# Token rows turned by VectorE in 32x32 squares, stored and gathered as four pieces a token

## The chip, the cores and the metric

The kernel runs on one core of a Trainium2 chip. The metric is the device time of one execution in microseconds; three runs of the kernel before gave 716.85, 718.15 and 718.57 us, so its median is 718.15 us. All data is float32.

## What is computed

Sliding-window attention with ALiBi biases, and behind it a mixture of experts that sends each token to one expert. Cut to what matters:

```python
# attention: 8 batches, 8 heads, 576 positions, 64 per head
mask = (rel >= 0) & (rel < 128)                    # rel = query position - key position
attn = softmax(where(mask, q @ k.T / 8 - slope[h] * |rel|, -1e9))
x = (attn @ v) as rows of (batch, position)        # 4608 tokens x 512
# experts: 8, each 512 -> 1024 -> 512
logits = x @ w_gate                                # 4608 x 8
e = argmax(logits, 1);  g = softmax(logits)[e]
y[t] = g[t] * (relu(x[t] @ w1[e]) @ w2[e])
```

## The kernel before, in words

**Order.** One instruction stream for each engine, in an order that is written out by hand (`manual_schedule`). What the program issues first for an engine runs first on it, so an instruction that waits holds up all that stands behind it on its engine. Two lists of small functions, `tasks` and `fill`, are dealt out between the large steps: `some()` and `step()` each take one entry (itself a list of functions) from the front.

**Attention** (lines 1192 to 1228). 4 pairs of batches (`bp`) x 4 pairs of heads (`hp`) make 16 units of 4 steps, so 64 steps `i`. In a step, TensorE computes the scores of step i+2 (L749), ScalarE takes their exponential (L755), VectorE multiplies by the bias factors (L758, L763), and TensorE multiplies the probabilities of this step with the values (L784). Twice a unit `finish` copies the result into `xT[bp]` (ScalarE, L801 and L803; features on partitions, 1152 tokens in columns) and sums the probabilities (TensorE L816 into a bank of the two-bank pool `ps_m`, VectorE L827 into `sumT`). One pool of two PSUM banks, `ps_m`, serves all the small products.

**Routing of a pair of batches** is dealt out over the 16 steps of the next pair, by `behind(bp)`: `gate` (L836, L841) and `turn` (L860) give gate logits with tokens on partitions; `scale_a`, `scale_b`, `scale_c` (VectorE, L869 to L923) give the softmax sums, the chosen expert and for each token and head one scale, into `K["ext"]`; `count`, `place` (L930, L939), `ones_at` (L968 to L977) and `enlist` (L987, L994) put the token's number into its expert's list. 9 tiles of 128 tokens (`TPB`) are made into rows meanwhile.

**Rows.** `row_turned` turns a tile of 128 tokens with four TensorE transposes (L1001) into a bank of `ps_m`, and ScalarE copies it into `xs` (L1003; pool `rows`, three buffers). `row_out` adds the 16 columns of scales on GpSimd (L1007) and stores rows of 528 numbers from SP's queue (L1009) to `x_rows` in device memory. 36 tiles in all.

**Gathering.** `index` turns lists of token numbers into `g_idx` (rows to read) and `s_idx` (rows to write). `gather` (L1107) issues one indirect DMA on GpSimd for each tile of 128 listed tokens; 39 in all: 4 for each of the 8 experts' fixed groups and 7 for single-tile further groups. `to_scale` (VectorE, L501) multiplies by the scales into `xn`, `to_columns` turns the tile with four TensorE transposes (L1124) into `ps_m`, and ScalarE copies it to `xgT` (L1125). `x_sums` (L537 to L540) and `w1_sums` (L529 to L532) make the sums that Strassen's scheme needs. For expert 0 only the tokens of the first three pairs of batches are taken in the fixed group (`gather(fixed[0], ...)`, the last entry of `behind(2)`), so that its products can begin while the last pair is being routed; its `w1_sums` run in units 10 and 11.

**Experts.** A fixed group of 512 tokens is multiplied by w1 in `strassen1` (seven products m, each in two halves c; 14 steps, L1295) and by w2 in `strassen2` (14 steps, L1352); after each step one `fill` entry is issued. A further group of 128 tokens is done plainly (L1391, L1407). Groups alternate: one fixed, one further. The scaled results are scattered by indirect DMAs (L1375). `with_tail` deals out the routing of the last pair of batches in `strassen1` of the first group, and the gather and preparation of the second group in its `strassen2`; later groups are gathered ahead of `strassen1` and prepared during `strassen2` of the group before.

Of the kernel before, what the change touches and what calls it, by code (L numbers as in the profile page):

```python
# [8 lines left out]
F32 = mybir.dt.float32  # L9
# [6 lines left out]
P = 128  # L16
# [441 lines left out]
def kernel(  # L458
# [36 lines left out]
    RW = Dm + 16  # L495

    x_d = nc.dram_tensor("x_rows", (N, RW), F32, kind="Internal").ap()

    def token_scales(to, rows):

        nc.vector.tensor_tensor(  # L501
            to.rearrange("p (h d) -> p h d", h=H), rows[:, :Dm].rearrange("p (h d) -> p h d", h=H),
            rows[:, Dm : Dm + H].unsqueeze(2).to_broadcast([P, H, D]), op=ALU.mult,
        )

    with ExitStack() as fast:
# [12 lines left out]
        rows = pool(tail, "rows", 3, side="right")  # L519
# [131 lines left out]
        far = ac.tile([P, 2, GC], F32, name="far")  # L651
# [50 lines left out]
        def route_consts():  # L702
# [12 lines left out]
            K["first_w"] = iota("first_w", [P, E], [[-1, E]], E, 0)  # L715
            K["off"] = iota("off", [P, E], [[NS * P, E]], -1, 0)

        def token_numbers():
# [3 lines left out]
            K["ext"] = rte.tile([P, NT, 16], F32, name="ext")  # L722
            nc.gpsimd.memset(K["ext"][:], 0.0)
# [125 lines left out]
        gsr, r_of, pr_of, ex_of, sel_of, pre_of, slot_of = {}, {}, {}, {}, {}, {}, {}  # L849
# [65 lines left out]
        def scale_c(bp):  # L915
            ts = slice(bp * TPB, (bp + 1) * TPB)
# [5 lines left out]
            nc.vector.reciprocal(gw[:], gw[:])  # L922
            nc.vector.tensor_tensor(  # L923
                K["ext"][:, ts, :H].rearrange("p t (h a) -> p t a h", a=2), r[:],
                gw[:].unsqueeze(2).unsqueeze(3).to_broadcast([P, TPB, 2, HP]), op=ALU.mult,
            )

# [36 lines left out]
        def ones_at(bp):  # L964
# [11 lines left out]
            orow = small.tile([P, TPB, P], F32, name="orow")  # L976
# [21 lines left out]
        def row_turned(bp, t):  # L998
            ps = ps_m.tile([P, 512], F32, name="m")
            for hp in range(HP):  # L1000
                nc.tensor.transpose(ps[:, hp * P : (hp + 1) * P], xT[bp][:, hp, t * P : (t + 1) * P], ident[:])  # L1001
            xs = xs_of[bp, t] = rows.tile([P, RW], F32, name="xs")
            nc.scalar.copy(xs[:, :Dm], ps[:])  # L1003

        def row_out(bp, t):
            xs = xs_of.pop((bp, t))
            nc.gpsimd.tensor_copy(xs[:, Dm:], K["ext"][:, bp * TPB + t, :])  # L1007
            for p0, n, r0 in placed(bp, t):
                nc.sync.dma_start(x_d[r0 : r0 + n, :], xs[p0 : p0 + n, :])  # L1009
# [526 lines left out]
```

## Time and profile before

| what | value |
|---|---|
| median of three runs | 718.15 us (716.85 to 718.57) |
| the profiled execution | 721.43 us |
| its span in the trace | 719.7 us |
| TensorE busy | 681.8 us, 6204 matmuls |
| VectorE busy | 343.9 us, 659 instructions |
| ScalarE busy | 225.8 us, 410 instructions |
| GpSimd busy | 112.4 us, 199 instructions |
| DMA | 122.01 MB in 59710 packets, 170 GB/s on average |

The span is what the trace shows from the first instruction to the last; the profiled execution's own time is 1.7 us longer. A line of a group gives the engine, the operation, what is written and read, the count, then the engine's busy time in that group and the mean duration of one, and the idle time just before these instructions with what ended it. Consecutive instructions of an engine overlap a little, so the distance from one to the next can be smaller than a duration. The first fixed group's first product begins at 191.99 us; from 255.3 us on a fixed and a further group together take 64.7 us, seven times over.

### The profile page before, as it was taken

The numbers are of one execution on the slowest core, as the hardware profiler recorded it, in microseconds if no ns is written. First come the engines' busy times: TensorE is split into PE (matmuls) and PEld (weight loads), VectorE is DVE, ScalarE is ACT, GpSimd is POOL, SyncE is SP. The second block draws the span as 40 slices with busy tenths as digits, with TensorE's granted clock in tenths as the row PEclk, the third lists the DMA queues.
The fourth block names the chain that finished last, engine by engine and source line by source line (L and its number), as shares of the span: only waits on it lengthen the run. The fifth ranks groups of instructions, "written<-read, shape, count | busy, mean of one in ns | idle before, by whom it ended". The sixth has DMA issues, their size and how long they took to land.

```text
span 719.7 us, 14743 instructions
## 1 busy us (share of the span) xinstructions
PE 681.8 (95%) x6204; PEld 569.5 (79%) x6204; DVE 343.9 (48%) x659; ACT 225.8 (31%) x410; POOL 112.4 (16%) x199
## 2 busy tenths in 40 slices
PE   6999799979899999999999999999999999999992
PEld 5878678767588888878897887889788888878881
DVE  4558449665558665524553443364254425514310
ACT  5655455444343223213302320331132023213110
POOL 7000101002001140122023002302200230210020
PEclk9999899989999999999999999999999999999997
DMA  8777877764415763184358218533823673182010
GB/s 241 209 215 237 260 225 206 229 175 143 164 75 193 279 242 117 31 296 172 117 169 312 79 55 291 201 117 97 309 93 116 211 278 117 36 297 108 1 61 6
DMA packets 59710, 122.01 MB, mean 170 GB/s; under 512 B 3857, under 2 KB 23345, under 8 KB 59634
## 3 DMA queue, kind: packets, MB, share of 16 engines
q1 hardware_dynamic: 52178, 100.08, 42.7%
q0 software_dynamic: 6304, 20.00, 7.5%
q8 instruction: 51, 0.84, 0.5%
q10 hardware_dynamic: 1152, 0.88, 0.4%
q14 instruction: 25, 0.20, 0.1%
HBM read 101.79 MB, written 19.96 MB: 169 GB/s over the span
## 4 chain that ended last, share of the span: by engine, by line
issue 57%; PE 19%; POOL 10%; DVE 6%; DMA 4%; ACT 2%; POOLq 0%; SPq 0%; DVEq 0%; ACTq 0%
POOL out_dram L1375 5%; PE sp L749 5%; POOL xg L1107 5%; PE at L784 4%; PE m L816 3%; PE m L1001 2%; DVE pe L758 2%; DMA q_sb<-in_qT_dram 2%; PE m L987 1%; PE m L836 1%; ACT pe L755 1%; DMA x_rows<-xs 1%; DMA out_dram<-zo,s_idx 1%; PE pair0b L1295 1%; PE pair0a L1295 1%
## 5 line engine op out<-in xcount | busy, mean ns | idle before, releaser
L1375 POOL DMA_INDIRECT out_dram<-zo,s_idx x39 | 43.9, 1126 | 383.6 <-DVE zo L1366 283.4
L758 DVE TENSOR_TENSOR pe<-pe,fac 128x768 f32<-128x768 f32 x48 | 45.9, 956 | 54.8 <-ACT pe L755 54.8
L749 PE MATMUL sp<-q_sb,k_sb 64*64 64x192 f32 (+2 forms) x1152 | 60.8, 328 | 6.2 <-DMA q_sb<-in_qT_dram 5.4
L755 ACT ACTIVATE pe<-sp 128x768 f32<-128x768 f32 x64 | 51.9, 811 | 45.9 <-PE sp L749 37.6
L784 PE MATMUL at<-pe,v_sb 64*64 64x192 f32 (+2 forms) x1408 | 61.2, 288 | 2.4 <-issue 1.6
L749 PEld LDWEIGHTS sp<-q_sb,k_sb 64*64 64x64 f32 x1152 | 42.7, 141 | 16.0 <-issue 5.1
L784 PEld LDWEIGHTS at<-pe,v_sb 64*64 64x64 f32 x1408 | 46.4, 136 | 11.3 <-issue 6.1
L1107 POOL DMA_INDIRECT xg<-x_rows,g_idx x39 | 42.7, 1095 | 29.8 <-DVE tb L1030 12.6
L1007 POOL COPY xs<-ext 128x16 f32<-128x16 f32 x36 | 12.4, 356 | 180.0 <-DVE ext L923 79.4
L816 PE MATMUL m<-pe,ind 128*32 128x192 f32 (+2 forms) x704 | 30.8, 295 | 6.0 <-ACT xs L1003 4.3
L1125 ACT COPY xgT<-m 128x512 f32<-128x512 f32 x39 | 22.9, 586 | 37.3 <-PE m L1124 36.4
L1306 ACT ACTIVATE h<-h 128x512 f32<-128x512 f32 x32 | 20.2, 631 | 39.5 <-DVE h L1305 32.1
L1003 ACT COPY xs<-m 128x512 f32<-128x512 f32 x36 | 20.6, 584 | 34.4 <-PE m L1001 16.1
L816 PEld LDWEIGHTS m<-pe,ind 128*32 128x32 f32 x704 | 24.2, 113 | 8.4 <-ACT xs L1003 4.4
L501 DVE TENSOR_TENSOR xn<-xg 128x512 f32<-128x512 f32 x39 | 26.2, 686 | 7.0 <-PE m L1124 6.0
L1124 PE MATMUL m<-ident,xn 128*128 128x128 f32 x156 | 23.6, 274 | 2.1 <-DVE xn L501 2.1
L1124 PEld LDWEIGHTS m<-ident,xn 128*128 128x128 f32 x156 | 19.1, 141 | 6.6 <-DVE xn L501 1.4
L1001 PE MATMUL m<-ident,xT 128*128 128x128 f32 x144 | 22.9, 294 | 1.4 <-DVE sumT L827 0.8
L1001 PEld LDWEIGHTS m<-ident,xT 128*128 128x128 f32 x144 | 17.1, 150 | 5.1 <-issue 2.2
L1407 PE MATMUL pair2a<-w,h 128*128 128x512 f32 x48 | 21.1, 592 | 0.0
L801 ACT COPY xT<-at 128x640 f32<-128x640 f32 (+1 forms) x32 | 18.7, 585 | 4.2 <-PE at L784 3.3
L537 DVE TENSOR_TENSOR xs<-xgT 128x512 f32<-128x512 f32 x8 | 5.5, 693 | 27.1 <-ACT xgT L1125 27.1
(355 smaller groups left out, 1371.5 us busy)
## 6 DMA issues: line engine op xcount, KB each, us to landing
w<-in_moe_w_dram SPq DMA_DIRECT2D x29, 2048.0 KB
k_sb<-in_kT_dram SPq DMA_DIRECT2D x15, 576.0 KB
q_sb<-in_qT_dram SPq DMA_DIRECT2D x15, 576.0 KB
v_sb<-in_v_dram SPq DMA_DIRECT2D x30, 288.0 KB
x_rows<-xs SPq DMA_DIRECT2D x32, 264.0 KB
w<-in_moe_w_dram SPq DMA_DIRECT2D x4, 512.0 KB
x_rows<-xs SPq DMA_DIRECT2D x8, 132.0 KB
pace<-pe SPq DMA_DIRECT2D x65, 0.0 KB
```

Source lines behind the costliest of these rows:

```text
L501: nc.vector.tensor_tensor(to.rearrange("p (h d) -> p h d", h=H), rows[:, :Dm].rearrange("p (h d) -> p h d", h=H), rows[:, Dm : Dm + H].uns ...
L749: nc.tensor.matmul(sp[c * KB : (c + 1) * KB, r, c0 : c0 + n], lhsT=k_sb[u][hs, c, kb * KB : (kb + 1) * KB], rhs=q_sb[u][hs, c, kb * KB : k ...
L755: nc.scalar.activation(pe[:], sp[:, :, :GC], AF.Exp, scale=SCALE)
L758: nc.vector.tensor_tensor(pe.rearrange("p r (k c) -> p r k c", k=2), pe.rearrange("p r (k c) -> p r k c", k=2), fac[:, h0 : h0 + 2, None, ...
L784: nc.tensor.matmul(acc[r * D : (r + 1) * D, c, lo - q0 : hi - q0], lhsT=v_sb[u][c * KB : (c + 1) * KB, kb, r * D : (r + 1) * D], rhs=pe[c ...
L816: nc.tensor.matmul(sm[32 * j : 32 * j + 32, lo - q0 : hi - q0], lhsT=none[:] if pe is None else ind[:, hp, :], rhs=fac[:, 0, :KB] if pe is ...
L1001: nc.tensor.transpose(ps[:, hp * P : (hp + 1) * P], xT[bp][:, hp, t * P : (t + 1) * P], ident[:])
L1107: nc.gpsimd.indirect_dma_start(out=g["xg"][:, j, :], out_offset=None, in_=src, in_offset=bass.IndirectOffsetOnAxis(ap=g_idx[:, g["c0"] + j ...
L1124: nc.tensor.transpose(tp[:, db * P : (db + 1) * P], xn[:, db * P : (db + 1) * P], ident[:])
L1125: nc.scalar.copy(g["xT"][:, :, j * P : (j + 1) * P], tp.rearrange("p (d q) -> p d q", d=DB))
L1375: ins = nc.gpsimd.indirect_dma_start(out=out[:, :], out_offset=bass.IndirectOffsetOnAxis(ap=s_idx[:, g["c0"] + j : g["c0"] + j + 1], axis= ...
L1407: nc.tensor.matmul(ps[:], lhsT=g["h"][:, fb, :], rhs=g["w2"][:, fb, :], start=(fb == 0), stop=(fb == FB - 1),)
```

## The change

The transposes leave TensorE. VectorE's own transpose turns squares of 32x32 where they stand, so a tile of 128 tokens x 512 features becomes four squares in each quarter of the partitions: partition 32a+j of `xs[:, k]` holds token 32k+j, and of it the features whose number within 128 lies in quarter a. So a token is stored as four **pieces** of 128 features and 4 scales (132 numbers, 528 bytes) that lie 64 rows apart in `x_pieces`. The gather fetches for each tile four times 128 pieces (`g_idx` gets four columns a tile, by a small product with the constant `to_squares` and six VectorE operations in `pieces`), so that each 32x32 square can be turned back by VectorE straight into `xgT`. The scales are brought onto the right partitions by `spread` (four small products and two ScalarE copies a pair of batches). Rows are stored by GpSimd's queue, one DMA a tile; `rows` has four buffers. The order of the entries changes in `behind`, `with_tail` and the fill of the first `strassen2`; `count_all` is split (`check_all` gets its last part, unchanged); and `prepare(fixed[0])` is issued as a whole at step 61, instead of entry by entry from step 61 on.

```diff
-        rows = pool(tail, "rows", 3, side="right")
+        rows = pool(tail, "rows", 4, side="right")
...
+            sq = K["to_squares"] = rte.tile([P, NA, P], F32, name="to_squares")
...
-                K["ext"][:, ts, :H].rearrange("p t (h a) -> p t a h", a=2), r[:],
-                gw[:].unsqueeze(2).unsqueeze(3).to_broadcast([P, TPB, 2, HP]), op=ALU.mult,
-            )
+                es[:], r[:], gw[:].unsqueeze(2).unsqueeze(3).to_broadcast([P, TPB, 2, HP]), op=ALU.mult,
+            )
+
+        def spread(bp):
+
+            n = TPB * H
+            ps = ps_m.tile([P, 512], F32, name="m")
+            for k in range(NA):
+                nc.tensor.matmul(
+                    ps[:, k * n : (k + 1) * n], lhsT=K["to_squares"][:, k, :],
+                    rhs=es_of[bp].rearrange("p t a h -> p (t a h)"), start=(k == 0), stop=True, skip_group_check=True,
+                )
+            ext = ext_of[bp] = small.tile([P, TPB, NA, HP], F32, name="ext")
+            v = ps[:, : NA * n].rearrange("p (k t a h) -> p a t k h", k=NA, t=TPB, a=2)
+            for a in range(2):
+                nc.scalar.copy(ext[a * KB : (a + 1) * KB], v[a * KB : (a + 1) * KB, a])
...
         def row_turned(bp, t):
-            ps = ps_m.tile([P, 512], F32, name="m")
-            for hp in range(HP):
-                nc.tensor.transpose(ps[:, hp * P : (hp + 1) * P], xT[bp][:, hp, t * P : (t + 1) * P], ident[:])
-            xs = xs_of[bp, t] = rows.tile([P, RW], F32, name="xs")
-            nc.scalar.copy(xs[:, :Dm], ps[:])
+            xs = xs_of[bp, t] = rows.tile([P, NA, PW], F32, name="xs")
+            nc.vector.transpose(
+                xs[:, :, :PD].rearrange("p k (h f) -> p k h f", h=HP),
+                xT[bp][:, :, t * P : (t + 1) * P].rearrange("p h (k j) -> p k h j", j=TQ),
+            )
 
         def row_out(bp, t):
             xs = xs_of.pop((bp, t))
-            nc.gpsimd.tensor_copy(xs[:, Dm:], K["ext"][:, bp * TPB + t, :])
-            for p0, n, r0 in placed(bp, t):
-                nc.sync.dma_start(x_d[r0 : r0 + n, :], xs[p0 : p0 + n, :])
+            nc.gpsimd.tensor_copy(xs[:, :, PD:], ext_of[bp][:, t])
...
+            nc.gpsimd.dma_start(
+                x_blocks[:, b0 : b0 + db + 1 : db, :], xs.rearrange("p (b k) w -> p b (k w)", b=2),
+            )
...
+        def pieces(cols, nm):
+
+            n = cols.stop - cols.start
+            ps = ps_m.tile([P, 512], F32, name="m")
+            for k in range(NA):
+                nc.tensor.matmul(
+                    ps[:, k * n : (k + 1) * n], lhsT=K["to_squares"][:, k, :], rhs=at_of[nm][:],
+                    start=(k == 0), stop=True, skip_group_check=True,
+                )
...
         def gather(g, src):
             nm = "" if g["n"] == NJ else "1"
-            g["xg"] = g["pool"].tile([P, g["n"], RW], F32, name="xg" + nm)
+            g["xg"] = g["pool"].tile([P, g["n"], NA, PW], F32, name="xg" + nm)
             for j in range(g["n"]):
-                nc.gpsimd.indirect_dma_start(
-                    out=g["xg"][:, j, :], out_offset=None, in_=src,
-                    in_offset=bass.IndirectOffsetOnAxis(ap=g_idx[:, g["c0"] + j : g["c0"] + j + 1], axis=0),
-                )
+                for k in range(NA):
+                    nc.gpsimd.indirect_dma_start(
+                        out=g["xg"][:, j, k, :], out_offset=None, in_=src,
+                        in_offset=bass.IndirectOffsetOnAxis(ap=g_idx[:, g["c0"] + j, k : k + 1], axis=0),
+                    )
...
         def to_columns(g, j):
...
-            tp = ps_m.tile([P, 512], F32, name="m")
-            for db in range(DB):
-                nc.tensor.transpose(tp[:, db * P : (db + 1) * P], xn[:, db * P : (db + 1) * P], ident[:])
-            nc.scalar.copy(g["xT"][:, :, j * P : (j + 1) * P], tp.rearrange("p (d q) -> p d q", d=DB))
+            nc.vector.transpose(
+                g["xT"][:, :, j * P : (j + 1) * P].rearrange("p h (k j) -> p k h j", j=TQ), g["xn", j][:],
+            )
...
             if bp == 2:
-                return [g3, t3, a, b + [lambda: row_turned(bp, 0)], c + n + [lambda: row_out(bp, 0)], p + rs[1:3], o + rs[3:5], e + rs[5:7], [early_table] + rs[7:9],
-                        [lambda: gather(fixed[0], x_d[: 3 * 2 * S, :])]]
...
+                return [g3, t3, a, b, c + n + turned[0:1], p + d + outs[0:1] + rs[1:2], o + rs[2:4],
+                        e + [lambda: index(first, listed[:, 0, :NJ], "0")] + rs[4:6],
+                        [early_table, lambda: pieces(first, "0")] + rs[6:9],
+                        [lambda: gather(fixed[0], x_d[: 3 * 2 * S * NA, :])]]
+            return [g3[0:1], g3[1:2], g3[2:] + t3[0:1], t3[1:], a, turned[0:1], b, turned[1:2], c + n,
+                    d + outs, p, rs[2:4], o, rs[4:6], e + rs[6:7], rs[7:9]]
...
-            if u == len(units) - 1 and g == 1:
-                tasks.extend(t for _, t in prepare(fixed[0]))
             if g != 2:
                 some()
+            if i + AHEAD == NG - 1:
+                while tasks:
+                    some()
+                tasks.extend(t for _, t in prepare(fixed[0]))
+                while tasks:
+                    some()
...
+                a, b, c + n, early[0:2], early[2:3] + w[0], p + d + [lambda t=t: row_out(bp, t) for t in range(3)],
+                w[1] + rs[3:4], o, rs[4:6], e + rs[6:8], [table_fixed] + rs[8:9], [lambda: pieces(rest, "1")] + w[2],
             ]
-            self_late.extend(w[6] + w[7])
+            self_late.extend(w2s[3:8])
...
+                for todo in (
+                    [lambda: gather(f1, x_d[:, :]), self_late[0], self_late[1]], [self_late[2], count_all],
+                    [self_late[3], check_all], [self_late[4], table_further], [next_groups],
+                    w1s[0:2], [lambda: pieces(slice(E * NJ, NC), "2")] + w1s[2:4], tokens[0], w1s[4:6], tokens[1], w1s[6:8], tokens[2], [], tokens[3],
+                    later(lambda: x_sums(f1), 4),
+                ):
+                    fill.append((f1, todo))
```

In `to_scale` the product keeps its size (128x512) and its new layout is that of the pieces. `tokens[j]` is `to_scale` and `to_columns` of tile j.

## The prediction, as it was put on record

> **What bounds the kernel now.** I read the page first, then the busy times by stretch, then single stretches in order of time.
>
> ```profile
> span 719.7 us, 14743 instructions
> ...
> PE 681.8 (95%) x6204; PEld 569.5 (79%) x6204; DVE 343.9 (48%) x659; ACT 225.8 (31%) x410; POOL 112.4 (16%) x199
> ...
> L1107 POOL DMA_INDIRECT xg<-x_rows,g_idx x39 | 42.7, 1095 | 29.8 <-DVE tb L1030 12.6
> ...
> L501 DVE TENSOR_TENSOR xn<-xg 128x512 f32<-128x512 f32 x39 | 26.2, 686 | 7.0 <-PE m L1124 6.0
> L1124 PE MATMUL m<-ident,xn 128*128 128x128 f32 x156 | 23.6, 274 | 2.1 <-DVE xn L501 2.1
> ...
> L1001 PE MATMUL m<-ident,xT 128*128 128x128 f32 x144 | 22.9, 294 | 1.4 <-DVE sumT L827 0.8
> ```
>
> TensorE is busy 95% of the span, and the transposes that go are 46.5 us of that. But 48% for VectorE is an average over unlike stages. The busy times by stretch (bounds, length, then PE, PEld, DVE, ACT, POOL, granted clock, DMA) show it:
>
> ```profile
> 56.70:93.40 36.70, 32.29 (x648) 26.76 (x648) 22.04 (x55) 17.67 (x31) 3.24 (x9) 0.91 0.84 255
> ...
> 105.10:136.50 31.40, 30.44 (x679) 25.68 (x671) 27.39 (x63) 17.25 (x31) 3.66 (x9) 1.00 0.75 216
> ...
> 196.40:255.30 58.90, 57.02 (x309) 50.03 (x305) 39.70 (x112) 18.49 (x37) 9.79 (x16) 1.00 0.50 177
> ...
> 320.00:384.70 64.70, 64.70 (x326) 54.55 (x325) 28.03 (x46) 15.47 (x29) 11.42 (x10) 1.00 0.50 172
> ```
>
> In the expert stage (last line) TensorE is never idle and VectorE has half its time free. While the second pair of batches is routed (second line) VectorE works 27.39 of 31.4 us. In the first line TensorE stands 4.26 us (at 71.4, for a ScalarE row copy that waits for the store of `xs`) and then runs at a lower clock:
>
> ```profile
> 75.60:79.00 3.40, 3.35 (x40) 2.59 (x44) 1.31 (x2) 1.84 (x5) 0.20 (x1) 0.50 0.97 313
> ...
> 154.50:158.00 3.50, 3.50 (x30) 3.05 (x34) 2.29 (x10) 1.21 (x3) 1.03 (x3) 0.50 0.33 92
> ```
>
> The clock is 0.50 after that wait and after a 3.7 us wait at 150.8, for some 6.8 us each time: a wait of that length costs 3.4 us more.
>
> **The sizes.** A square transpose on VectorE is not in the trace. Its nearest row is L501, the same 128x512 numbers, at 0.69 us, and 0.60 from start to start in a row of them. Below lies 0.47 (a one-input operation of 128x384 took 355 ns, scaled by 512/384), above 1.35, the longest row of VectorE (L977). I take 0.60 in a chain, the row of the same size. The Trainium skill, "VectorE: DVE Perf Modes", "The three transpose paths", gives 311 ns for 128x128 in bf16 and only squares of 32; four of these would make 1.24 us, an estimate from that page alone, no run here shows it, and it speaks against this change: by it my sum below would end some 17 us above the kernel before.
>
> Four TensorE transposes hold the queue for 0.435 us between other products (241.88 to 242.32 us), and about 0.62 us in the attention (0.66 at 62.06). A small product with `to_squares` is like L987 (18 in 2.18 us): 0.12 us; 16 in `spread` and 12 in `pieces` add 3.4 us. An indirect DMA has a pitch on GpSimd of 1.27 us:
>
> ```profile
> 177.01 1.09 POOL L1107 DMA_INDIRECT xg<-x_rows,g_idx  x1 [5.91 <-DVE pe L758]
> 178.40 0.98 POOL L1107 DMA_INDIRECT xg<-x_rows,g_idx  x1 [0.30 <-issue]
> 179.68 0.95 POOL L1107 DMA_INDIRECT xg<-x_rows,g_idx  x1 [0.30 <-issue]
> 180.94 0.95 POOL L1107 DMA_INDIRECT xg<-x_rows,g_idx  x1 [0.30 <-issue]
> ```
>
> With 2112 and with 2048 bytes a row it is the same (1095 and 1126 ns), so I take it to go with the 128 rows and keep 1.27 for 528 bytes; ends: 0.5 (if a part goes with bytes) and 1.7 (the longest pitch, beside VectorE's work). So a 512-token gather takes 16 x 1.27 = 20.3 us instead of 5.1.
>
> A plain DMA from GpSimd took 0.72 to 0.84 us (gate weights), at most an indirect one's 1.47. With the 0.36 us scale copy, 36 stores are some 42 us on an engine that is idle there; SP's queue loses 40 stores, behind which its paced loads stood. The Trainium skill, "DMA: Bandwidth & Descriptors", "Issuing engine by pattern", calls the SP and ACT queues generally faster, which speaks against this move; with its first-byte figures (about 1 against 0.6 us) a store would land 0.4 us later, 0.4 us once in the sum (the last store before the gather). The trace shows SP's stores held long: a row copy waited 5.8 us for one.
>
> The 75 ScalarE copies (L1003, L1125: 43.5 us) go, off the path, and 8 small ones (like L803, 0.28) come. The constants add four GpSimd selections of at most 0.97 us in the first 20 us, needed after 60 us: nothing. `check_all` only moves.
>
> **Sum, by stage, against the profiled execution (721.43 us).**
>
> *First routed pair (to 93.4).* From 56.7 TensorE needs 32.29 - 3.4 (clock) - 9 x 0.62 + 0.5 = 23.8 us; VectorE 22.04 + 9 x 0.60 = 27.4, with some 2 us of gaps 29.5. VectorE sets the pace; 36.7 become 29.5: **-7.2**, mostly the wait and the slow clock. With four buffers and stores off SP's queue a store has three to four steps (7 to 10 us) to land, against 5.5 us for a DMA under load (the gather issued until 234.5 landed at 239.95).
>
> *Second pair (105.1 to 136.5).* VectorE 27.39 + 5.4 = 32.8 exceeds the 31.4 there are, since the weight sums of expert 0 fall here too: **+1.5**. TensorE's 5.1 us are not earned.
>
> *Third pair, up to the first expert group: the doubtful part.* Now `place` waits for VectorE at 154.5, and the first gather starts at 177.0. After the scan (154.35) VectorE has, up to the last row: nine turned rows 5.4, four probability products 3.5, two sums 0.8, `place` 1.8, `ones_at` 2.5, the list 0.2, `index` and `pieces` 2.2, `early_table` 0.5, together 17 us, and about 2 of waiting while TensorE is at half clock: 174. Copy, issue and landing add 3, so the gather starts at **177, as now** (174 to 180). TensorE's 5 us without rows are again not earned: `enlist` and `pieces` wait for VectorE.
>
> Then 16 DMAs: the 16th is issued by 177 + 20.3 = 197.3 and landed 2.3 us later (now: issued by 181.9, DMA quiet after 184), 199.6. `prepare(fixed[0])` is issued whole at step 61, ahead of the `sumT` additions of steps 62 and 63. So on VectorE they stand behind the last tile: scale and turn 1.25, four sums 2.4, `sumT` 0.9 make 204.2. TensorE's attention work ends by about 187; it does m=1's first half and then stands in `gate`, whose PSUM bank the `sumT` addition has to free.
>
> ```profile
> 191.99 1.89 PE L1295 MATMUL pair0a<-xgT,w 128*128 128x256 f32 x8
> 193.81 1.92 PE L836 MATMUL m<-xT,wgd 128*32 128x512 f32 x16
> ...
> 196.44 1.99 PE L1295 MATMUL pair0b<-xgT,w 128*128 128x256 f32 x8
> ```
>
> The gates take 2.6 us here, so the second half starts at 206.8 instead of 196.44: +10.4, and after such a wait half clock, +3.4: **+13.8**.
>
> *First group's rest.* 9 rows and 4 tiles leave TensorE: 13 x 0.435 = -5.7; 12 small products +1.4; VectorE's added 9 x 0.60 and six list operations, in a chain of adds and routing, +2 (0 to 6). The second gather, 20.3 us of a 24.2 us `strassen2`, lands some 30 us after its start, and the sums are needed at 24.2 + 4 x 1.73 = 31: just hidden. **-2.3**.
>
> *Later groups.* 24 fixed and 7 further tiles, 31 x 0.435: **-13.5**. Cover: 20 gathers are 25.4 us from the start of `strassen1` (24.2 us), and the tiles are turned in the second to fifth step of `strassen2`; VectorE rises from 28.0 to 31 of 62.5 us. If that cover went, VectorE would wait some 5 us a group, without TensorE, which needs its additions only late in `strassen2`.
>
> Sum: -7.2 + 1.5 + 13.8 - 2.3 - 13.5 = -7.7. The profiled execution would take 713.7; since it was 3.3 us above the median of the runs, I put the same difference on the median: 718.15 - 7.7 = **710.4 us**.
>
> **Rivals.**
> *The join is hidden:* pitch under 0.8 us, or gather begun 10 us earlier. Then +13.8 becomes about 0 to 2: 697. For it: ScalarE's copies are gone from the chain; against it: the equal prices of both kinds of indirect DMA.
> *TensorE bounds everywhere:* 36 x 0.62 + 39 x 0.435 - 3.4 = 35.9 us and the waits of 7.7: 675. Against it: the 27.39 of 31.4.
> *Slower: VectorE's transpose is dear.* Each 0.1 us more costs 27 x 0.1 in the attention, where VectorE sets the pace, and some 1.2 in the first group, 3.9 in all. From 0.80 us in a chain the gain is gone; at 1.0 the sum is +7.9 : 726; at 1.35 about 740. For it: no row shows this operation.
> *It does little:* the gathers under weight loads come late in each group too: 31 tiles' gain lost, 718 to 723.
>
> **Numbers.** Forecast 0.42 (703 to 717), hidden join 0.27 (692 to 702), everywhere 0.06, slower 0.20, little 0.05. The range 692 to 728 leaves out the 675 case and the dear end of the slower one. 0.3% is 2.2 us, about what a measurement can tell: faster 0.71, same 0.07, slower 0.22.
>
> **What would show it.** VectorE's transposes at 0.6 to 0.7 us; no half clock near 75; VectorE full from 105 to 136; TensorE idle some 10 us in `gate` before the second half of m=1, with GpSimd's 16 DMAs before it; 62.5 us for each later pair of groups. A gather pitch far from 1.27, or `sumT` ahead of the tiles, would prove me wrong.

## The result: 0.7% slower, and the profile after

The changed kernel takes 722.20 us (median of seven runs, 721.68 to 725.28) beside 718.15 us for the kernel before on the same chip: a ratio of 1.0073, 95% interval 1.0053 to 1.0092. The prediction was 710.4 us and faster. On two other chips the changed kernel took 769 and 770 us, 6.5 to 6.7% more than the kernel before; that is a second matter, and the last group of experiments is about it. Each ratio is taken on one chip.

The page of the changed kernel: the span and the engines' busy times.

```profile
span 721.9 us, 14376 instructions
...
PE 661.7 (92%) x5960; PEld 552.2 (76%) x5960; DVE 394.7 (55%) x749; ACT 186.2 (26%) x343; POOL 256.0 (35%) x360
```

TensorE lost 20 us of work, but the span did not get shorter: it is idle or at half clock for longer. The groups of the new instructions (count, then busy us and mean ns of one, then idle time ahead of them) show that their sizes were as assumed:

```profile
L1165 POOL DMA_INDIRECT xg<-x_pieces,g_idx x156 | 157.7, 1011 | 57.0 <-issue 46.3 <-DVE pick L1118 7.3 <-DMA x_pieces<-xs 2.7
L1184 DVE STREAM_TRANSPOSE xgT<-xn 128x512 f32<-128x512 f32 x39 | 27.7, 711 | 1.3
L1034 POOL DMA_DIRECT2D x_pieces<-xs x36 | 26.3, 730 | 43.0 <-DVE xs L1022 31.6 <-POOL xs L1029 7.2 <-issue 4.2
L1022 DVE STREAM_TRANSPOSE xs<-xT 128x512 f32<-128x512 f32 x36 | 23.8, 689 | 0.4 <-DMA x_pieces<-xs 0.4
```

A transpose on VectorE takes 0.69 to 0.71 us, an indirect DMA 1.0 us with 0.3 us behind it (a pitch of 1.25 us, whether a row has 2112 or 528 bytes), a store from GpSimd 0.73 us. The estimate of 1.24 us from the Trainium skill's page "VectorE: DVE Perf Modes", "The three transpose paths", is not what this kernel shows.

Where the time went, stage by stage (the times are those of the first gates, of the second half of m=1, of the second group's m=1, of the first and last further tile and of the last scatter in the two traces):

| stage | before | after | difference | predicted |
|---|---|---|---|---|
| start to the first pair's gates | 44.03 | 43.38 | -0.7 | 0 |
| first pair routed | 49.29 | 44.70 | -4.6 | -7.2 |
| second pair routed | 43.18 | 48.56 | +5.4 | +1.5 |
| third pair, to the second half of m=1 | 59.94 | 74.66 | +14.7 | +13.8 |
| first group's rest | 58.85 | 56.14 | -2.7 | -2.3 |
| second group, to its further tile | 50.67 | 54.67 | +4.0 | -2.2 (5 tiles x 0.435) |
| the rest, to the last scatter | 401.45 | 390.02 | -11.4 | -11.3 (26 x 0.435) |
| sum | | | +4.7 | -7.7 |

Behind the last scatter the kernel before has 12.3 us and the changed one 9.8, which nothing in the change explains; the profiled executions so differ by 2.3 us (721.43 and 723.74).

Three places in the trace carry the difference. First, the two stretches of the attention, in products of TensorE (the first pair of batches, then the second):

```profile
64.92 0.77 PE L793 MATMUL at<-pe,v_sb 64*64 64x192 f32 x16 [0.56 <-DVE pe L767]
67.67 1.23 PE L941 MATMUL m<-es,to_squares 128*128 128x72 f32 x8 [1.98 <-DVE es L932]
109.60 0.77 PE L793 MATMUL at<-pe,v_sb 64*64 64x192 f32 x16 [1.38 <-DVE pe L767]
112.86 1.98 PE L941 MATMUL m<-es,to_squares 128*128 128x72 f32 x8 [2.48 <-DVE es L932]
```

`spread` stands on TensorE right behind `scale_c`, so it waits for VectorE's `es`, 1.98 us in the first pair and 2.48 us in the second. What follows each is half clock (the column of 0.50 in the busy times by stretch), 3.4 us in the first pair and 10.2 us in the second, whose first 6.8 us are:

```profile
113.00:116.40 3.40, 3.40 (x36) 3.07 (x38) 1.47 (x3) 1.24 (x3) 0.55 (x2) 0.50 0.85 214
116.40:119.80 3.40, 3.40 (x46) 2.43 (x42) 0.98 (x2) 0.81 (x1) 1.52 (x4) 0.50 0.98 302
```

Second, the join of attention and experts, whose sum came out within a microsecond of the predicted one: TensorE waits for the tiles, does half of m=1, and then stands in the gates for `sumT`, which VectorE has behind the last tile.

```profile
196.06 3.75 PE L1360 MATMUL pair0a<-xgT,w 128*128 128x256 f32 x8 [11.93 <-DVE xgT L1184]
207.30 4.07 PE L845 MATMUL m<-xT,wgd 128*32 128x512 f32 x24 [7.49 <-DVE sumT L836]
211.30 2.24 PE L1360 MATMUL pair0b<-xgT,w 128*128 128x256 f32 x8
```

Third, the second group's gather. Its indices are written by 245.9 us, but it begins 8 us after the last row's store, and TensorE reaches m=6 of the group before the sums are there:

```profile
241.96 0.73 POOL L1034 DMA_DIRECT2D x_pieces<-xs  x1 [0.92 <-DVE xs L1022]
249.99 1.51 POOL L1165 DMA_INDIRECT xg<-x_pieces,g_idx  x1 [7.30 <-DVE pick L1118]
```

```profile
277.49 3.75 PE L1360 MATMUL pair2a<-xs,ws 128*128 128x256 f32 x8 [2.99 <-DVE xs L538]
```

The 3.75 us for eight products that take 1.89 elsewhere is half clock again.

### The profile page after: what moved, and what is told of

The parts are those of the page before. It is cut to its first block, busy times and chain, and to the rows that moved or that the text cites. A ratio compares the mean times of both kernels' runs of the same rounds, so it can differ in the third digit from the quotient of the medians.

```text
span 721.9 us, 14376 instructions
## 1 busy us (share of the span) xinstructions
PE 661.7 (92%) x5960; PEld 552.2 (76%) x5960; DVE 394.7 (55%) x749; ACT 186.2 (26%) x343; POOL 256.0 (35%) x360
## 4 chain that ended last, share of the span: by engine, by line
PE 58%; issue 17%; DVE 12%; POOL 9%; DMA 2%; ACT 1%; POOLq 0%; ACTq 0%; DVEq 0%
POOL xg L1165 7%; PE sp L758 4%; PE pair2a L1360 3%; PE pair2b L1360 3%; PE pair0b L1360 3%; PE pair0a L1360 3%; PE pair0b L1417 3%; PE pair0a L1417 3%; PE pair1b L1417 3%; PE pair1a L1417 3%; PE at L793 3%; PE pair1b L1360 3%; PE pair1a L1360 3%; PE pair2b L1417 2%; PE pair2a L1417 2%
## 5 line engine op out<-in xcount | busy, mean ns | idle before, releaser
L1165 POOL DMA_INDIRECT xg<-x_pieces,g_idx x156 | 157.7, 1011 | 57.0 <-issue 46.3
L1034 POOL DMA_DIRECT2D x_pieces<-xs x36 | 26.3, 730 | 43.0 <-DVE xs L1022 31.6
L1360 PE MATMUL pair0a<-xgT,w 128*128 128x256 f32 x72 | 18.9, 410 | 11.9 <-DVE xgT L1184 11.9
L1184 DVE STREAM_TRANSPOSE xgT<-xn 128x512 f32<-128x512 f32 x39 | 27.7, 711 | 1.3
L1360 PEld LDWEIGHTS pair0a<-xgT,w 128*128 128x128 f32 x72 | 14.6, 206 | 15.1 <-issue 13.0
L1022 DVE STREAM_TRANSPOSE xs<-xT 128x512 f32<-128x512 f32 x36 | 23.8, 689 | 0.4 <-DMA x_pieces<-xs 0.4
L537 DVE TENSOR_TENSOR w2s<-w 128x512 f32<-128x512 f32 x16 | 11.0, 686 | 20.5 <-DMA w<-in_moe_w_dram 20.5
L845 PE MATMUL m<-xT,wgd 128*32 128x512 f32 (+1 forms) x96 | 11.5, 584 | 8.7 <-DVE sumT L836 7.5
```

The costliest lines, as they stand in the source:

```text
L1034: nc.gpsimd.dma_start(x_blocks[:, b0 : b0 + db + 1 : db, :], xs.rearrange("p (b k) w -> p b (k w)", b=2),)
L1165: nc.gpsimd.indirect_dma_start(out=g["xg"][:, j, k, :], out_offset=None, in_=src, in_offset=bass.IndirectOffsetOnAxis(ap=g_idx[:, g["c0"] ...
L1184: nc.vector.transpose(g["xT"][:, :, j * P : (j + 1) * P].rearrange("p h (k j) -> p k h j", j=TQ), g["xn", j][:],)
L1360: nc.tensor.matmul(ps[:, f * 256 : (f + 1) * 256], lhsT=left[m][:, d, fb * P : (fb + 1) * P], rhs=right[m][:, d, :], start=(m in (1, 2, 5) ...
```

## The experiments

Theory: TensorE's saved work is given back at three separate waits: the join, the wait of `spread`, and the late second gather. Main rivals: the transposes load VectorE everywhere; the 16 DMAs alone make the join dear, whatever the order.

**The join: order and length.** `e1_join` issues the last pair's gates and turns ahead of the first group's tiles:

```diff
-                tasks.extend(t for _, t in prepare(fixed[0]))
-                while tasks:
-                    some()
...
         load_w2(fixed[0], w2_a)
+        for k in range(3):
+            gate(BP - 1, k)
+        for k in range(3):
+            turn(BP - 1, k)
+        tasks.extend(t for _, t in prepare(fixed[0]))
         while tasks:
             some()
...
-                [lambda k=k: gate(bp, k) for k in range(3)], [lambda k=k: turn(bp, k) for k in range(3)],
+                [], [],
```

> The gates and turns of the last pair of batches are issued ahead of the first expert group's tiles, so that no VectorE instruction that TensorE's gates need stands behind the gather. All else is the changed kernel (722.2 us; first half of m=1 at 196.06 us, second half at 211.30, m=6 at 218.32 in its trace). Theory (the order on VectorE's queue, with the 16 DMAs, makes the join dear): gates done by 189 us, second half of m=1 at about 200, m=6 at about 207 to 208, where the last tile's sums set it; 8 to 11 us less, 711 to 714 us, faster than the kernel before. Rival 1 (the 16 DMAs alone make the join dear, the order is worth nothing): second half of m=1 still at 206 or later, at most 2 us less, 720 to 722. Rival 2 (the loss lies in VectorE's own transposes, everywhere a little): no more than 3 us less.

Measured: 713.14 us, ratio to the kernel before 0.9929 (0.9904 to 0.9954). TensorE in this run:

```profile
188.94 2.65 PE L845 MATMUL m<-xT,wgd 128*32 128x512 f32 x24
...
200.94 3.41 PE L1357 MATMUL pair0a<-xgT,w 128*128 128x256 f32 x8 [7.26 <-DVE xgT L1184]
204.19 1.89 PE L1357 MATMUL pair0b<-xgT,w 128*128 128x256 f32 x8
...
209.38 1.89 PE L1357 MATMUL pair0a<-xs,ws 128*128 128x256 f32 x8
```

The gates no longer wait, and m=6 comes at 209.38 instead of 218.32, although this execution reached the join some 4 us later. Against the changed kernel's 1.0073 the gain is 1.4%, some 10 us: the order on VectorE's queue was the larger part of the join, and rivals 1 and 2 of this run fall. `e2_quarter` leaves the order and takes 12 of the 16 DMAs away (`for k in range(1 if g is fixed[0] else NA)`, the rest of `xg` set to zero early).

> Leaves out 12 of the 16 indirect DMAs of the first group's gather (three of four pieces of each of its tokens are zeros); order and all else as in the changed kernel. Theory (pitch of 1.25 us times 16, and behind it the chain on VectorE): 15 us less gather; last tile at about 188 us instead of 202.75, sums done by 193, second half of m=1 at about 197 instead of 211.3; some 14 us less, 707 to 710. Rival (the gather's bytes or landing set the time, not the number of instructions on GpSimd): first tile lands no sooner than 189, gain under 6 us, 716 to 719.

Measured: 711.03 us, ratio 0.9908 (0.9877 to 0.9939), some 12 us less than the changed kernel. The last tile was turned at 192.9 instead of 203.5, m=6 came at 207.67 instead of 218.32. Less than expected, since the four landings still took until 192.2; the length counts, not only the order. Either repair alone frees most of the 14.7 us.

**The wait of `spread`.**

```diff
-            ..., b, turned[1:2], c + n,
-                    d + outs, p, rs[2:4], ...
+            ..., b, turned[1:2], c + n,
+                    [], d + outs + p, rs[2:4], ...
```

> For the first two pairs of batches the four small products that spread the scales stand one step of the attention later, beside those of the list places; all else is the changed kernel. Theory (TensorE stands there for VectorE's scales, and the wait costs half clock too): no wait of 2 us or more near 65 and 110 us, no half clock at 68 and at 113 us, the third pair's first gate at 130 to 133 us instead of 136.64; 4 to 6 us less, 716 to 718. Rival 1 (VectorE is simply full there, the wait moves to the next product): half clock somewhere else in the same stretch, at most 1.5 us less, 720.5 to 722. Rival 2 (the clock falls whatever TensorE waits for): half clock for as long as before, no gain.

Measured: 717.94 us, ratio 1.0014 (0.9988 to 1.0040), so 0.6% or 4.3 us less than the changed kernel. `spread` does not wait any more, and the third pair's gates begin at 133.12 instead of 136.64:

```profile
114.98 1.11 PE L941 MATMUL m<-es,to_squares 128*128 128x72 f32 x8
```

There is no half clock between 45 and 150 us in this execution. The first pair takes 41.4 us and the second 44.5: -7.9 and +1.3 against the kernel before, where the prediction had -7.2 and +1.5. That agreement is partly luck. This execution's first gates came late, at 47.22 us instead of 43.38, behind a 3.0 us wait in the first 41 us, and the first pair made that up. Four runs further below have the same later spread (`all3`, `all3_2`, `all3_3`, `join_spread`). In these and this one the two pairs together took 85.9 to 91.6 us (mean 89.2 of five profiled executions), against 92.8 to 95.1 (mean 94.0) in eight profiled executions with the spread where the change put it. The prediction's two terms make it 86.8. So the wait of `spread` is worth some 5 us of the 7. In all five, TensorE still waits for VectorE's probabilities near the place where `spread` stood, and in `all3` half clock follows for 10.2 us, from 112.3 us on, as in the changed kernel:

```profile
109.33 0.77 PE L793 MATMUL at<-pe,v_sb 64*64 64x192 f32 x16 [1.32 <-DVE pe L767]
111.13 0.34 PE L793 MATMUL at<-pe,v_sb 64*64 64x64 f32 x8 [1.02 <-DVE pe L767]
```

So rival 1 of this run, that the wait moves to the next product, holds in part.

**The second gather.** One small load on SP's queue waits for the last row's store, ahead of the second group's weights:

```diff
+            last = 2 * (BP - 1) * NK + 8 + NK
+            no_earlier_than(x_blocks[0:1, last, 0:1])
             load_w1(fixed[1], lp["w"])
             load_w2(fixed[1], lp["w"])
```

> The two weight loads of the second expert group wait for the landing of the last token row's store (one small load on SP ahead of them); all else is the changed kernel, where the second gather began at 249.99 us, 4 us after its indices were there, and TensorE then stood 3.0 us for the group's sums and ran 6 us at half clock. Theory (the last store's landing is held up by the 4 MB of weights): second gather starts at 246 to 247, no half clock near 277, 5 to 6.5 us less, 716 to 717. Rival 1 (the gather waits for its indices, or for GpSimd): starts at 250 as before, no gain, 721.5 to 723. Rival 2 (the weights come late instead): TensorE or the weight sums wait for them, slower by 1 to 4 us.

Measured: 720.51 us, ratio 1.0036 (1.0018 to 1.0054): about 2.7 us less, with an interval that still touches the changed kernel's. The gather now starts 4.2 us behind the last store, not 8.0:

```profile
242.57 0.73 POOL L1034 DMA_DIRECT2D x_pieces<-xs  x1 [0.92 <-DVE xs L1022]
...
246.79 1.12 POOL L1165 DMA_INDIRECT xg<-x_pieces,g_idx  x1 [3.49 <-DVE g_idx L1083]
```

So the landing of that store was held up by the 4 MB of weights, although the page names another releaser (`pick`, long written). There is no half clock near 277, TensorE's wait for the sums is 1.68 us instead of 2.99, and the second group takes 50.4 instead of 54.7 us. The rest of the expected gain stays with that wait.

**VectorE's transposes in the attention.** On top of the later spread, 23 of the 27 row transposes are left out (those rows are stored with old contents).

> The kernel of the run with the later spread, without 23 of the 27 row transposes of the first three pairs of batches: their rows are stored with what the first four tiles left in the buffers. It asks whether VectorE's transposes set the pace of the attention, as the prediction had it. Against the run with the later spread (717.94 us; third pair's first gate at 133.12 us, first gather at 177.9): Theory (VectorE sets the pace in the second pair and in the third one's chain up to the gather): the second pair's window shrinks by 4 to 6 us, the first gather starts 5 to 9 us sooner, 5 to 10 us less in all, 708 to 713. Rival (TensorE and its waits set the pace, VectorE's 0.69 us each lie beside it): windows within 1.5 us of the other run's, 716 to 719.

> The attention without 23 of its 27 row transposes (rows stored with old contents), once more, since TensorE stood for instructions in the first run of it. Theory (VectorE's transposes set the pace): the second pair's window 3 to 6 us shorter than 44.5 us, the first gather 5 to 9 us sooner than 177.9, 708 to 713 us. Rival (they lie beside TensorE's work): 716 to 719. If the layout of instructions decides: 765 to 775 again.

Measured: 772.31 us and, on another chip, 762.39 us (ratios 1.0683, 1.0653 to 1.0714, and 1.0567, 1.0521 to 1.0613). Both fell on chips with the hold-up described below, so the totals tell nothing of the transposes. The attention does: the second pair took 41.5 and 41.4 us, against 43.5 to 46.9 in the five executions with the later spread and all transposes, and the first gather came at 169.82 and 167.76, against 176.07 to 179.45. In the second run:

```profile
167.76 1.06 POOL L1170 DMA_INDIRECT xg<-x_pieces,g_idx  x1 [3.58 <-DVE g_idx L1088]
```

The first pair did not shrink (47.8 and 44.5 us, beside 41.4 to 44.8). So VectorE's transposes set the pace from the second pair up to the gather, by some 9 us; a price of that size was in the prediction (5.4 us in each of two pairs).

**The stores alone.** The kernel before, with one word changed (`nc.sync.dma_start` to `nc.gpsimd.dma_start` in `row_out`):

> The kernel before, with the 40 stores of token rows issued on GpSimd's queue instead of SP's; nothing else of the change (TensorE's row transposes, rows of 528 numbers, three buffers stay). Theory (a store on SP's queue stands behind paced loads, and in the first pair TensorE waited 4.26 us for a buffer): the wait at 71.4 and the half clock at 75 go, 3 to 7 us less than the kernel before, 711 to 715. Rival 1 (the wait was for a buffer that a store of the same length frees on any queue): same wait, within 1.5 us of 718. Rival 2 (a GpSimd store lands later): longer waits in the attention, 719 to 723.

> The kernel before with its row stores on GpSimd's queue, on another chip: it gained 10.0 us beside the kernel before in its first runs, more than the 3 to 7 expected. If the gain belongs to the queue: 8 to 11 us less than the kernel before here too, a ratio of 0.985 to 0.989, whichever time the changed kernel has on this chip. If part of it belonged to that chip: 3 to 6 us less, 0.992 to 0.996.

> The kernel before, profiled once more, to see which part of its 10 us to the version with stores on GpSimd's queue is the wait at 71.4 us with its half clock, which part other waits, and which the stretch after the last scatter (12.3 us in its first profile, 5.5 in the other kernel's). If the queue's waits make it: the third pair's first gate and all later stages 4 to 8 us later than in the other kernel. If the end of the program makes it: the last scatter within 2 us of the other kernel's 706.3, and some 12 us behind it.

Measured: 713.06 us beside 723.09 (ratio 0.9858, 0.9833 to 0.9883), and on another chip 712.45 beside 722.06 (0.9869, 0.9828 to 0.9911). A new profile of the kernel before (median 724.68, ratio to itself 1.0017, 0.9977 to 1.0058), from the same chip as the first of these, has the wait on ScalarE's row copy that the prediction named; with the stores on GpSimd it is smaller (kernel before, then the other):

```profile
77.77 1.51 PE L816 MATMUL m<-pe,ind 128*32 128x64 f32 x24 [5.42 <-ACT xs L1003]
```

```profile
72.71 0.86 PE L816 MATMUL m<-pe,ind 128*32 128x64 f32 x24 [2.11 <-ACT xs L1003]
```

The first pair takes 45.8 instead of 50.4 us; the stages behind it differ by 3 to 4 us both ways, and up to the last scatter 4.5 us remain (706.26 against 710.77), as expected. The other 6.7 us lie behind the last scatter: 12.2 us in the kernel before, 5.5 in this one, in both profiles of each. What runs there the trace does not show; this part stays open, so of the 11.2 us between these two executions less than half is explained. The Trainium skill, "DMA: Bandwidth & Descriptors", "Issuing engine by pattern", gives plain stores to Sync and calls that path generally faster; here the measurement decides for GpSimd in this program. The shorter wait for the stores accounts for the 4.5 us at most.

**Do the repairs add up? And 770 us.** Three repairs together, or two, with the entries of `with_tail` two steps earlier:

> The three repairs together on the changed kernel: gates and turns of the last pair ahead of the first group's tiles (and the entries behind them two steps earlier), the spread one step later, the weights of the second group behind the last row's store. Theory (three separate waits on the path): the gains add, 10 + 4 + 3 to 6 us less than the changed kernel's 722.2, 702 to 706, faster than the kernel before by 1.7 to 2.3%. Rival 1 (what one repair gains another wait takes: VectorE's routing chain of the last pair or the second gather sets the end): 709 to 713, no better than the first repair alone. Rival 2 (the entries two steps earlier run into the tiles' sums on VectorE): TensorE waits for the tokens' places and runs at half clock, 706 to 709.

> Two of the three repairs: gates and turns ahead of the tiles (entries behind them two steps earlier) and the later spread; the weights of the second group are loaded as in the changed kernel. Theory (separate waits, gains add): 10 + 4 us less than the changed kernel, 706 to 709, and with the second gather two steps earlier up to 3 less. Rival (one takes what the other gives): 711 to 714. If the layout of instructions decides, a time near 770 can come here too.

> The three repairs together once more. If the 770 us belong to the chip: 702 to 706 here, as expected the first time, unless the changed kernel itself takes 765 or more in these runs. If they belong to the layout of its instructions: 765 to 775 again, with the gaps at the start of each second layer.

> The changed kernel itself once more, beside the two runs below that took some 770 us with TensorE standing for its own instructions (gaps of 1 to 2 us put down to issue) at the start of each second layer. If those gaps belong to the kernels' own layout of instructions: 720 to 724 here, none of those gaps. If they belong to the chip on which they ran together with this kind of kernel: about 765 to 775 on that chip, and as before on another.

> The three repairs together once more, for their sum. On a chip that holds the engines up during GpSimd's long rows of gathers: 765 to 775 again. On one that does not: gains of 10, 4 and 3 to 6 us added to the changed kernel's ratio of 1.007, so 0.979 to 0.985, some 703 to 707 us; if one takes what the other gives, 0.99 or more.

Measured: 770.58 (`all3`), 771.79 (`join_spread`), 769.12 and 764.25 us (`all3_2`, `all3_3`) for the repaired ones (ratios 1.0605, 1.0555 to 1.0654; 1.0666, 1.0616 to 1.0716; 1.0628, 1.0575 to 1.0681; 1.0599, 1.0540 to 1.0659) and 769.03 for the changed kernel itself (1.0674, 1.0627 to 1.0721). The expectation of 702 to 706 failed, but not for the reasons of its rivals: the changed kernel itself has two times, 722 us on one chip and 770 on others, and these runs had only chips of the second kind. Whether the three gains add stays open: it was not measured on the first kind, and on the second kind the hold-up already falls into the gather of the second group. In `all3_2`, during the last of those 16 DMAs and just behind them, VectorE stands 9.71 us (to 260.62), and the second group's first product comes at 273.08, later than the 265.86 of the changed kernel on the same chip.

**The hold-up.** On those chips a pair of later groups takes 66 to 70 us instead of 62.5. In the same executions the last pair, in which GpSimd has only 4 gathers left to issue, takes 62.5. Two stretches of 14 us in a pair of the changed kernel, the same distance from the start of GpSimd's row, first on such a chip and then on the first chip:

```profile
368.00:382.00 14.00, 11.23 (x47) 8.32 (x45) 1.51 (x3) 2.40 (x4) 8.51 (x9) 0.96 0.21 48
```

```profile
353.00:367.00 14.00, 14.00 (x66) 12.05 (x65) 10.97 (x19) 4.93 (x9) 8.66 (x9) 1.00 0.52 166
```

GpSimd does the same (8.5 and 8.7 us), VectorE a seventh, TensorE loses 2.8 us, and the DMA engines' share falls from 0.52 to 0.21. GpSimd is in the second half of its row of 20 gathers (353.4 to 379.2 us), and VectorE's additions wait for products that TensorE finished long before (`pair2a` at 370.2, `pair2b` at 372.1):

```profile
369.34 0.69 DVE L1382 TENSOR_TENSOR h<-pair2b,u 128x512 f32<-128x512 f32 x1 [1.21 <-ACT h L1385]
376.51 0.69 DVE L1370 TENSOR_TENSOR h<-pair2a,u 128x512 f32<-128x512 f32 x1 [6.47 <-PE pair0b L1360]
382.18 0.69 DVE L1370 TENSOR_TENSOR h<-pair2b,u 128x512 f32<-128x512 f32 x1 [4.98 <-remote]
```

A late load of instructions is an obvious rival. Against it: between 358 and 388 us of this execution no packet of the queues that load instructions was moved, and the engines went on all the same.

Four kernels on one chip of this kind. `e9_plain` loads three of four pieces by SP, `nc.sync.dma_start(g["xg"][:, j, k, :], src[r0 : r0 + P, :])`; `e10_pause` puts twelve small `memset`s on GpSimd behind each five gathers; `e11_train` adds to the kernel before

```diff
+                for k in range(3 if more else 0):
+                    nc.gpsimd.indirect_dma_start(
+                        out=junk[:, (3 * j + k) % 7, :], out_offset=None, in_=x_q,
...
```

> The changed kernel, to show which of its two times the chip of these four runs gives: 720 to 725, or 764 to 772 as on two of the four chips so far, with 70 us instead of 62.5 for a pair of later groups and TensorE standing for no shown reason while GpSimd issues the last of its 20 gathers.

> In the later groups three of a tile's four indirect DMAs are plain loads of 128 consecutive pieces from SP's queue (so those groups' numbers are other tokens'): the same pieces and bytes, 5 indirect DMAs on GpSimd a pair of groups instead of 20. Theory (a long row of indirect DMAs on GpSimd holds up the other engines on some chips): where the changed kernel takes 765 or more, this one takes 720 to 728, its pairs 62.5 us; where the changed kernel takes 722, the same within 3 us. Rival (the many small pieces in the DMA queues hold up the engines): as slow as the changed kernel on the same chip.

> In the later groups GpSimd works on a small scratch tile for about 3 us after each five indirect DMAs; nothing else is changed, 20 indirect DMAs a pair of groups. Theory (the engines are held up only after a dozen of them in a row, since in the trace of the slow chip the first 14 us of the row are undisturbed): on a slow chip most of the 47 us go, 722 to 740; on the other chips 722 to 728, as the tiles come 9 us later. Rival (the number in all counts, not the row): no better than the changed kernel on the same chip, or up to 5 us worse.

> The kernel before, with each later group's five indirect DMAs followed by three more each into a scratch tile (pieces of 192 bytes): 20 in a row on GpSimd a pair of groups, and nothing else of the change. Theory (the row of them alone is the cause): where the changed kernel takes 765 or more, the kernel before so altered loses 30 to 50 us too, 750 to 770; on other chips under 2 us. Rival (the pieces' layout, VectorE's transposes or the stores are the cause): within 2 us of the kernel before on every chip.

| kernel | us | ratio to the kernel before | a later pair, us |
|---|---|---|---|
| changed | 770.09 | 1.0650 (1.0592 to 1.0709) | 68.4 to 70.0 |
| plain loads instead of 15 of 20 | 728.19 | 1.0061 (1.0024 to 1.0098) | 62.5 |
| pauses in the row | 742.26 | 1.0280 (1.0231 to 1.0330) | 64.0 to 64.2 |
| kernel before with 15 more | 784.64 | 1.0852 (1.0811 to 1.0894) | 74.8 to 75.9 |

All four went the way of the theory, three of them past their ranges: 728.2 us for 720 to 728, 742.3 for 722 to 740, and 61 us lost by the last instead of 30 to 50. One pair of the last, beside one of the kernel before on the first chip (length, then TensorE, weight loads, VectorE, ScalarE, GpSimd):

```profile
317.30:392.90 75.60, 67.67 (x326) 56.30 (x325) 28.13 (x47) 15.16 (x29) 25.70 (x26) 0.93 0.46 151
```

```profile
306.00:370.70 64.70, 64.70 (x326) 54.55 (x325) 28.04 (x47) 15.47 (x29) 11.43 (x11) 1.00 0.49 171
```

The other engines have the same numbers of instructions; only GpSimd's row is longer. In that row VectorE waits 7.8 us and goes on 1.7 us after the row's last DMA was begun:

```profile
359.13 0.95 POOL L1115 DMA_INDIRECT junk<-x_rows,g_idx  x1 [0.31 <-issue]
```

```profile
360.81 0.69 DVE L1313 TENSOR_TENSOR h<-pair2b,u 128x512 f32<-128x512 f32 x1 [7.80 <-remote]
```

So a row of some 20 indirect DMAs on GpSimd holds up the other engines on these chips, not the pieces, their bytes or VectorE's transposes; and a row broken after every five does so much less. That it shows only in the second half of a row, from about the tenth to the sixteenth DMA on, is read from the traces. What inside the chip is in the way was not found. Nor was it found why some chips are free of it: of the five chips with a number on record four showed it (0, 3, 7 and 13) and one did not (15), and neither did the chip of the result, whose number is not on record. No chip with a number ran such rows at two different times, so something that changes with time is not ruled out. The kernel before differs as well, a little: 718 us on the free chips, 721 to 724 on the others.

## Why the prediction was wrong

- **TensorE's savings** were right: each later pair takes 62.5 us, and -11.4 was measured for -11.3.
- **Sizes** were right: 0.69 to 0.71 us for a transpose (0.60 in a chain), 1.25 for the pitch of a gather, 0.73 for a store. The rival of a dear transpose did not come, although the time came out on its side. The time also fell into the 718 to 723 us of the rival "it does little", by chance: its cause, late gathers in each group, is excluded by the later pairs.
- **The join** had the right mechanism, the gates behind the tiles on VectorE's queue, and a sum that two errors brought near: +14.7 for +13.8. The gather started at 180.8 instead of 177, 3.8 us late; half clock, priced at 3.4, cost about 1.5, since most of it fell into TensorE's waiting (the gates took 4.1 us instead of 2.6).
- **First failed step: the attention, "-7.2" and "+1.5".** The working said that in the second pair VectorE sets the pace and priced only its transposes; it did not ask what stands on TensorE's queue behind VectorE's last result. `spread` does, and behind TensorE's 2 to 2.5 us there come 13.6 us of half clock, which cost up to 6.8. The terms came out at -4.6 and +5.4. With `spread` one entry later the two pairs gained 4.8 us in the mean of all executions, where 7.2 us were missing (94.0, 89.2 and the prediction's 86.8). The rest stays with TensorE's waits for VectorE's probabilities and their half clock, which the working did not price either.
- **Second failed step: "just hidden".** The working let the second gather land some 30 us after `strassen2`'s start. Its first DMA began 8.7 us after that start, since the last row's store lands behind 4 MB of weights, and the last tile was there at 33. The working also compared the landing with the time at which the sums are needed, and left out scaling, turning and two sums in between: 2.9 us in the trace (274.45 to 277.34). A margin of 1 us was counted as none lost; it cost 3.0 us of wait and 3.4 of half clock. With the weights behind the store (`e6_weights`) 1.68 us of the wait stayed and the half clock went.
- Together these two stages differ by 12.7 us from the forecast (6.5 and 6.2); the other stages give 0.3 back, which makes the 12.4 us between the sum on record (-7.7) and the measured one (+4.7).
- **What nothing in it could have told:** the hold-up. The prediction asked only how long 16 or 20 gathers take, not what a long row of them does to the engines beside it; the trace of the kernel before has rows of five gathers.

## What to carry to other kernels

When work moves from one engine to another, list for each new instruction that waits what is queued behind it on its own engine, in every stage where it is issued; here two lines of order were worth 10 and 4 us. A transfer that is "just hidden" should be priced as late, with half clock behind it. And one part of a change can be worth more than the whole: the stores on GpSimd's queue alone make the kernel before 1.3 to 1.4% faster on two chips, although more than half of that gain is not explained, and by its ratio (0.986 and 0.987) that version is ahead of both kernels.

## What the runs showed of the hardware

- **Half clock comes in pieces of 3.4 us.** Its stretches in all traces, but for the last of each, which the program's end cuts, last 3.4, 6.8, 10.2, 13.7, 17.1, 20.5 or 23.9 us, and the same wait of `spread` in the second pair brought 10.2 us in one execution and 3.4 in another. The Trainium skill, "TensorE: Matmul & The Clock Gate", "Part 1: The HAM clock gate (the "warmup" mystery)", gives a free-running window of 3413 ns, which fits; it puts the fall behind at least one idle window, but here 0.56 and 1.98 us of waiting within 3.3 us (to 67.67) were enough.
- **A long row of indirect DMAs on GpSimd can hold up all other engines**, on some chips and not on others: 20 in a row cost 4 to 8 us in each pair of later groups of the changed kernel and its repaired versions, and 10 to 11 us in the kernel before with 15 more.
- **The time behind the last scatter belongs to the program**: 12.3, 9.8 and 5.5 us for three kernels (before, changed, stores on GpSimd's queue), the same within 0.1 us in each of their profiles.
